# Batch 0 of an attention-and-mixer kernel: the w_tok2 matmuls read their moving operand contiguously, and the identity matmuls write PSUM with a step of four

## The chip, the cores and the metric

The kernel runs on one core of a Trainium2 chip. The metric is device time in microseconds: 292.88 us before the change, the median of three runs from 292.81 to 293.12. One further execution was profiled; it took 292.57 us, and the span in its trace, from the first to the last instruction, is 290.8 us. Its TensorE ran at a granted clock of 0.997.

## The reference

The inputs are eight batches of eight heads with 576 tokens of 64 values. A Performer attention comes first, then an MLP-mixer block on its output.

```python
# attention, per batch and head
phi(x) = exp(h - max(h)) / sqrt(128),  h = (x*scale) @ omega.T - |x*scale|^2 / 2
kv  = phi(k).T @ v ;  z = sum over tokens of phi(k)
x   = (phi(q) @ kv) / (phi(q) @ z + 1e-6)        # heads side by side: x is [576, 512]
# mixer, per batch
h   = relu(x.T @ w_tok1) @ w_tok2                # [512, 576], token mixing
u   = x + h.T                                    # [576, 512]
out = u + relu(u @ w_ch1) @ w_ch2                # channel mixing, d_ch = 1536
```

The sizes that matter below: w_tok2 is [256, 576], and of the 576 tokens of a batch the first 512 are handled apart from the last 64.

## The kernel before, in words

Everything is in fp16 in SBUF, with fp32 sums in PSUM. There are eight PSUM banks: six single ones, of which each step takes one or two (`bank`), and two used as a pair (`pair`). The 512 main tokens of a batch lie on 128 partitions by 4: token 4p + j is on partition p, at index j (`NJ` = 4). The last 64 tokens ("tails") are handled for two batches together.

For each batch the stages are: attention (`attention`, lines 498 to 719), which ends with VectorE dividing numerators by denominators into the tile x (L700, L701); token mixing; and channel mixing (`channel_mix`, L813 to L873), which runs 12 blocks of w_ch1 (L822), a relu on ScalarE (L839) and 12 blocks of w_ch2 for each of four groups of tokens (L855).

Channel mixing needs u with the features on partitions (`uT`). Batches 1 to 7 compute u with the tokens on partitions (`token_mix`, L721 to L758): w_tok2 is the stationary operand (L745), r1 the moving one, VectorE adds x (L748), and a DMA transposes the result (L753). Batch 0 has its own version, `token_mix_first` (L760 to L795), which gets uT straight from TensorE. For each of the four blocks of 128 features:

- L771 and L772 compute x.T @ w_tok1, ten matmuls of 128 columns, and a relu (L778 on ScalarE or L780 on VectorE) leaves r1.
- L787 runs four matmuls with x[:, j] as stationary operand and the identity as moving operand, which put the transposed x into the four quarters of one bank, quarter j holding the tokens 4c + j.
- L789 runs two matmuls of 512 columns on top, with r1 stationary and w_tok2 moving. `w2_of(tb)` gives w_tok2's columns in the order of these quarters: first all columns 4c, then all 4c + 1 and so on. So two neighbours in the stream are four fp16 values, 8 bytes, apart in SBUF.
- L793 casts the bank to fp16 into uT, on ScalarE for three blocks and on VectorE for one.

In batch 0 the residual u is added in channel mixing too: four identity matmuls with uT as stationary operand (L853) go between the w_ch2 matmuls. VectorE copies the sum to the fp32 tile `o` (L861), and SP stores it (L869), 128 rows of 2 KB, each fourth row of the batch's output.

The order of the work on each engine is written when the program is built. A planner (`Planner`) is given jobs, each with an engine, an assumed cost, a due key, its dependencies and the buffers it takes and gives; it plays them through and emits each engine's instructions in the order that comes out. Where TensorE would idle in the head of the kernel it puts in matmuls on zeros (L908). The head, up to about 28 us, holds batch 0's attention and token mixing; in it batch 1's k is transposed on TensorE as well (L465, L485), and the first feature maps of batch 1's keys follow (L611). Loads of batch 1 and of the weights are issued by POOL (L316, L334, L427 for w_ch1, L442 for w_ch2).

Of the kernel before, what the change touches and what calls it, by code (L numbers as in the profile page):

```python
# [37 lines left out]
class Planner:  # L38
# [20 lines left out]
    def add(self, eng, cost, key, fn, deps=(), take=(), give=(), rows=False, wire=0.0):  # L59
        job = Job(eng, cost, key, fn, [d for d in deps if d is not None], list(take), list(give), rows, wire)  # L60
        for g in job.give:
            self.left[g] = self.left.get(g, 0) + 1
        self.jobs.append(job)
        return job
# [108 lines left out]
    def place(self, tag, name):  # L173
        return self.held[tag, name]
# [3 lines left out]
def kernel(  # L178
# [12 lines left out]
    nc = tc.nc  # L191
# [6 lines left out]
    P = 128  # L198
    SM = 512
    ST = S - SM  # L200
    NJ = SM // P
    NT = DT // P
# [13 lines left out]
    def sb(shape, dt, name):  # L216
        return pool.tile(shape, dt, name=name)
# [14 lines left out]
    ident16 = sb([P, P], FP16, "ident16")  # L232
# [6 lines left out]
    w2 = sb([P, NT, S], FP16, "w2")  # L239
# [46 lines left out]
    def bank(name):  # L286
        return banks[place("bank", name)]
# [7 lines left out]
    def mm(n, cols):  # L295
        return n * (cols / 2400.0 + 0.0025)
# [7 lines left out]
    def dma(eng, key, wire, fn, deps=(), take=(), give=(), cost=None):  # L304
        cost = (0.75 if eng == "POOL" else 0.45) if cost is None else cost
        job = add(eng, cost, key, fn, deps, take, give, wire=wire)
        if eng == "POOL":
            job.after = issued[-1] if issued else None
            issued.append(job)
        return job  # L310
# [97 lines left out]
    def pads():  # L408
# [6 lines left out]
        out=w1m.rearrange("p j t -> p (j t)"), in_=moe_w_tok1[0:SM, :].rearrange("(p j) t -> p (j t)", j=NJ)))  # L415
# [2 lines left out]
        j_w1t.append(dma("POOL", key, 0.2, cost=0.58, fn=lambda: nc.gpsimd.dma_start(out=w1t[o * ST : (o + 1) * ST, o, :], in_=moe_w_tok1[SM:S, :]), deps=[j_w1tz]))  # L418
    load_w1t(0, HEAD["w1t"])
    j_w2 = dma("POOL", HEAD["w2"], 1.7, lambda: nc.gpsimd.dma_start(out=w2, in_=moe_w_tok2.rearrange("(i p) s -> p i s", p=P)))  # L420
    def w2_of(tb, j=None):
        rows = w2[:, tb, 0:SM].rearrange("p (c j) -> p j c", j=NJ)
        return rows if j is None else rows[:, j, :]
    j_wc1 = []
    def load_wc1(i):
        c0 = i * (DC // 2)
# [13 lines left out]
    for i in range(2):  # L440
        c0 = i * (NCB // 2)
        j_wc2.append(dma("POOL", -3.0 + 0.1 * i, 3.85, lambda c0=c0: nc.gpsimd.dma_start(  # L442
            out=wc2[:, c0 : c0 + NCB // 2, :], in_=moe_w_ch2[c0 * P : (c0 + NCB // 2) * P, :].rearrange("(i p) d -> p i d", p=P))))
# [3 lines left out]
        out=omega16.rearrange("p (i d) -> p i d", i=2), in0=omega_nat.unsqueeze(1).broadcast_to((P, 2, D)), scalar1=c_scale, scalar2=None, op0=ALU.mult), deps=j_om)  # L447
# [312 lines left out]
    def token_mix_first(b, key, step, jx):  # L760

        jrs, uT = [], []
        for db in range(ND):
            cols = slice(db * P, (db + 1) * P)
            n = ("h1", b, db)
            def t1(n=n, cols=cols):
                x = t_x[place("x", b)]
                for tb in range(NT):
                    ps = bank(n)[:, tb * P : (tb + 1) * P]
                    for j in range(NJ):  # L770
                        nc.tensor.matmul(ps, w1m[:, j, tb * P : (tb + 1) * P], x[:, j, cols], start=(j == 0), stop=False)  # L771
                    nc.tensor.matmul(ps, w1t[:, b % 2, tb * P : (tb + 1) * P], x[:, NJ, cols], start=False, stop=True)  # L772
            j1 = add("PE", mm(10, P), HEAD["t1"][db], t1, deps=[*jx[2 * db : 2 * db + 2], j_w1, j_w1t[b % 2]], take=[("bank", n), ("r1", b)])
            re_act, uo_act = BY["re"][db] == "A", BY["uo"][db] == "A"
            def relu(n=n, cols=cols, re_act=re_act):
                o, i = t_r1[place("r1", b)][:, :, cols], bank(n)[:, 0 : NT * P].rearrange("p (t c) -> p t c", t=NT)
                if re_act:
                    nc.scalar.activation(out=o, in_=i, func=AF.Relu)  # L778
                else:
                    nc.vector.tensor_relu(out=o, in_=i)  # L780
            jr = add("ACT" if re_act else "DVE", 0.3 if re_act else 0.38, HEAD["re"][db], relu, deps=[j1], give=[("bank", n)])
            jrs.append(jr)
            n2 = ("uT", b, db)
            def ut_(n2=n2, cols=cols):
                ps, x, r1 = bank(n2), t_x[place("x", b)], t_r1[place("r1", b)]
                for j in range(NJ):
                    nc.tensor.matmul(ps[:, j * P : (j + 1) * P], x[:, j, cols], ident16, start=(j == 0), stop=False, skip_group_check=True)  # L787
                for tb in range(NT):
                    nc.tensor.matmul(ps, r1[:, tb, cols], w2_of(tb), start=False, stop=(tb == NT - 1), skip_group_check=True)  # L789
            j2 = add("PE", mm(2, 512) + mm(4, P), HEAD["ut"][db], ut_, deps=[jr, j_w2, j_ident], take=[("bank", n2), ("uT", b)], give=[("x", b), ("r1", b)])  # L790
            def ut_out(db=db, n2=n2, uo_act=uo_act):
                o, ps = t_uT[place("uT", b)][:, :, db, :], bank(n2).rearrange("p (j c) -> p j c", j=NJ)
                (nc.scalar.copy if uo_act else nc.vector.tensor_copy)(out=o, in_=ps)  # L793
            uT.append(add("ACT" if uo_act else "DVE", 0.5 if uo_act else 0.69, HEAD["uo"][db], ut_out, deps=[j2], give=[("bank", n2)]))
        return jrs, uT  # L795
# [17 lines left out]
    def channel_mix(c, key, jt):  # L813
# [27 lines left out]
        for j in range(NJ):  # L841
            last = c == B and j == NJ - 1
            for hf in range(2 if last else 1):
                n = ("h4", c, j, hf)
                cols = slice(hf * (DM // 2), (hf + 1) * (DM // 2)) if last else slice(0, DM)
                prev = None
                for part in range(3):
                    def c2(j=j, part=part, n=n, cols=cols):
                        ps, r3 = bank(n), t_r3[place("r3", c)]
                        for cb in range(4 * part, 4 * part + 4):  # L850
                            if c == 0 and cb == NCB - 1:
                                for db in range(ND):
                                    nc.tensor.matmul(ps[:, db * P : (db + 1) * P], t_uT[place("uT", c)][:, j, db, :], ident16,  # L853
                                                     start=False, stop=False, skip_group_check=True)
                            nc.tensor.matmul(ps[:, cols], r3[:, cb, j * P : (j + 1) * P], wc2[:, cb, cols], start=(cb == 0), stop=(cb == NCB - 1))  # L855
                    prev = add("PE", mm(4, 256 if last else 512) + (mm(4, P) if c == 0 and part == 2 else 0.0), key + 0.5 + 0.5 * (3 * j + part) / 12 + 0.2 * hf, c2,
                               deps=[prev, *jr[4 * part : 4 * part + 4], *j_wc2], take=[("bank", n)], give=[("r3", c)] + ([("uT", c)] if c == 0 else []))
                k2 = key + 0.5 + 0.5 * (3 * j + 3) / 12
                def oadd(j=j, n=n, cols=cols):
                    if c == 0:  # L860
                        nc.vector.tensor_copy(out=t_o[place("o", (c, j))], in_=bank(n))  # L861
                        return
                    uu = t_u[place("u", c)][:, j, :] if c < B else ut[j]
                    nc.vector.tensor_tensor(out=t_o[place("o", (c, j))][:, cols], in0=uu[:, cols], in1=bank(n)[:, cols], op=ALU.add)  # L864
                jo = add("DVE", 0.4 if last else 0.69, k2, oadd, deps=[prev], take=[("o", (c, j))], give=[("bank", n)] + ([("u", c)] if 0 < c < B else []))
                def store(j=j, cols=cols, last=last):
                    o = t_o[place("o", (c, j))]
                    if c < B:
                        nc.sync.dma_start(out=out[c, 0:SM, :].rearrange("(p j) d -> p j d", j=NJ)[:, j, :], in_=o)  # L869
                    else:  # L870
                        for i in range(2):
                            (nc.scalar if j >= 2 and i else nc.sync).dma_start(out=out[2 * j + i, SM:S, cols], in_=o[i * ST : (i + 1) * ST, cols])
                dma("SP", k2, 0.65, store, deps=[jo], give=[("o", (c, j))], cost=0.4 if c < B else 0.8)  # L873

    for i in range(4):
# [65 lines left out]
```

The softmax here doesn't subtract the row's maximum and nothing guards it: scores larger than these inputs give would overflow.

## Time and profile before

| What | Before |
|---|---|
| Timed runs | 292.88 us (292.81 to 293.12) |
| Profiled span | 290.8 us |
| DVE (VectorE) busy | 145.3 us, 50% |
| ACT (ScalarE) busy | 155.9 us, 54% |
| POOL (GpSimd) busy | 90.6 us, 31% |
| L853, identity matmuls writing contiguously, duration | 219 ns |
| L793 on ScalarE, cast of one bank | 586 ns |
| Batch 0's stores L869, first issue | 59.8 us |

A page of the profile gives busy times of each engine, then the chain of work that ended last, followed back from the end of the kernel. The durations of single matmuls overlap, since the next one starts while the one before it drains: L853's 219 ns is the time from start to end of one matmul, while four of them in a row take 0.22 us in the chain. To price a matmul that is followed closely by others, the chain or the distance between starts is read. PEld is TensorE loading the stationary operand, which runs beside the matmul before it.

### The profile page before, as it was taken

How to read it: one execution, taken by the hardware profiler on the slowest of the kernel's cores; microseconds unless marked ns; L12 is line 12 of the kernel's file. 1: busy time of each engine (PE TensorE's matmuls, PEld its weight loads, DVE VectorE, ACT ScalarE, POOL GpSimd, SP SyncE). 2: the span in 40 equal slices, each digit the busy share in tenths (PEclk: the TensorE clock that was granted, in tenths of full speed). 3: DMA queues.
4: the chain of work that ended last, by engine and by line, in shares of the span. 5: the costliest groups of instructions: out<-in, count | busy, mean ns of one | idle time of the engine just before them, and what ended most of it. 6: DMA issues, size and time to landing. Idle time of an engine off the chain costs nothing.

```text
span 290.8 us, 5502 instructions
## 1 busy us (share of the span) xinstructions
PE 283.9 (98%) x2210; PEld 141.7 (49%) x2210; DVE 145.3 (50%) x269; ACT 155.9 (54%) x305; POOL 90.6 (31%) x115
## 2 busy tenths in 40 slices
PE   7899999999999999999999999999999999999994
PEld 3465454445544544465445544554455444444443
DVE  4885843558449533756567446646465242111011
ACT  5963992098457553865466636753765501621700
POOL 8995740128006501550165014601421000000000
PEclk9999999999999999999999999999999999999998
DMA  8999999699964996999769976897711033003004
GB/s 192 193 197 195 202 228 172 98 246 175 177 108 108 186 152 125 180 171 202 113 129 182 197 114 113 159 221 115 152 72 39 0 72 147 0 18 144 2 20 124
DMA packets 75737, 39.57 MB, mean 136 GB/s; under 512 B 54976, under 2 KB 70720, under 8 KB 75328
## 3 DMA queue, kind: packets, MB, share of 16 engines
q0 software_dynamic: 24304, 17.43, 41.2%
q1 hardware_dynamic: 50624, 21.01, 32.3%
q10 hardware_dynamic: 784, 0.79, 0.9%
q8 instruction: 17, 0.28, 0.4%
q14 instruction: 8, 0.07, 0.1%
HBM read 35.88 MB, written 16.52 MB: 180 GB/s over the span
## 4 chain that ended last, share of the span: by engine, by line
PE 95%; ACT 3%; DVE 0%; issue 0%; DVEq 0%; ACTq 0%
PE bank L855 33%; PE bank L822 32%; PE bank L745 4%; PE bank L728 4%; PE bank L611 3%; PE bank L657 3%; PE bank L625 2%; PE pair L691 2%; PE bank L908 2%; ACT kp L494 1%; PE bank L789 1%; PE bank L803 1%; PE bank L664 1%; PE bank L465 1%; PE bank L729 1%; ACT qp L494 1%
## 5 line engine op out<-in xcount | busy, mean ns | idle before, releaser
L839 ACT ACTIVATE r<-bank 128x512 f16<-128x512 f32 x108 | 64.5, 602 | 69.8 <-PE bank L822 69.8
L855 PE MATMUL bank<-wc,r 128*128 128x512 f16 (+1 forms) x444 | 101.5, 374 | 0.0
L822 PE MATMUL bank<-uT,wc 128*128 128x512 f16 x376 | 89.5, 379 | 0.0
L855 PEld LDWEIGHTS <-r 128*128 128x128 f16 x444 | 40.8, 98 | 46.9 <-issue 5.1
L822 PEld LDWEIGHTS <-wc 128*128 128x128 f16 x424 | 39.5, 98 | 42.6 <-issue 0.5
L637 DVE TENSOR_REDUCE km<-kp 128x8 f16<-128x1024 f16 x32 | 38.7, 1209 | 9.4 <-ACT kp L494 9.2
L494 ACT ACTIVATE qp<-bank 128x512 f16<-128x512 f32 x64 | 35.2, 620 | 13.4 <-PE bank L625 13.4
L494 ACT ACTIVATE kp<-bank 128x512 f16<-128x512 f32 x64 | 34.4, 610 | 8.9 <-PE bank L611 8.9
L644 POOL TENSOR_TENSOR vs<-v,vs 128x512 f16<-128x512 f16 x32 | 33.4, 1055 | 16.1 <-DVE vs L639 12.1
L864 DVE TENSOR_TENSOR o<-u,bank 128x512 f32<-128x512 f16 x28 | 19.1, 681 | 28.1 <-PE bank L855 28.1
L571 POOL TENSOR_TENSOR vbd<-vt,vbd 128x1024 f16<-128x1024 f16 x7 | 13.4, 1919 | 33.2 <-DVE vbd L562 21.7
L365 POOL COPY ktt<-kT 128x256 f16<-128x256 f16 x6 | 2.4, 396 | 68.4 <-DMA kT<-k 68.4
L701 DVE TENSOR_TENSOR x<-pair,rc 128x640 f16<-128x640 f32 x28 | 23.1, 824 | 1.0
L748 DVE TENSOR_TENSOR u<-x,bank 128x512 f16<-128x512 f16 x28 | 17.4, 682 | 9.1 <-PE bank L745 9.1
L700 DVE RECIPROCAL rc<-pair 128x10 f32<-128x10 f32 x28 | 6.0, 216 | 26.9 <-PE pair L693 26.9
L691 PEld LDWEIGHTS <-qp 128*128 128x128 f16 x256 | 12.8, 98 | 6.1 <-issue 0.7
L736 DVE TENSOR_SCALAR r<-bank 128x512 f16<-128x512 f32 x7 | 4.8, 692 | 19.5 <-PE bank L729 19.5
L728 PE MATMUL bank<-x,w1m 128*128 128x512 f16 x56 | 14.4, 379 | 0.0
L657 PEld LDWEIGHTS <-kp 128*128 128x128 f16 x256 | 10.9, 98 | 5.3 <-ACT qp L494 0.9
L657 PE MATMUL bank<-vs,kp 128*128 128x65 f16 x256 | 13.0, 193 | 0.4 <-ACT qp L494 0.4
L745 PE MATMUL bank<-r,w 128*128 128x512 f16 x56 | 13.2, 379 | 0.0
L611 PE MATMUL bank<-omT,kT 64*128 64x128 f16 x256 | 12.5, 218 | 0.1
(102 smaller groups left out, 267.8 us busy)
## 6 DMA issues: line engine op xcount, KB each, us to landing
out_dram<-o SPq DMA_DIRECT2D x32, 256.0 KB, 2.5
q<-in_q_dram POOLq DMA_DIRECT2D x6, 576.0 KB, 6.5
k<-in_k_dram POOLq DMA_DIRECT2D x6, 576.0 KB, 10.2
wc<-in_moe_w_ch_dram POOLq DMA_DIRECT2D x4, 768.0 KB, 10.3
v<-in_v_dram POOLq DMA_DIRECT2D x6, 512.0 KB, 6.3
r<-in_q_dram POOLq DMA_DIRECT2D x4, 256.0 KB, 7.2
v<-in_v_dram POOLq DMA_DIRECT2D x4, 256.0 KB, 7.2
out_dram<-o SPq DMA_DIRECT2D x5, 128.0 KB, 2.3
```

What stands on the lines that cost most here:

```text
L494: nc.scalar.activation(out=out, in_=in_, func=AF.Exp, bias=0.0, scale=1.0)
L611: nc.tensor.matmul(ps[e][:, c : c + M], m[half[e], r, :], omT[half[e]], start=True, stop=True)
L637: nc.vector.reduce_max(out=mx, in_=kpv, axis=AX.X)
L644: nc.gpsimd.tensor_tensor(out=vs[:, :, 0:D], in0=t_v[place("v", b)][:, hh[0] : hh[0] + 2, :].rearrange("p h (j d) -> p (h j) d", d=D), in1 ...
L657: nc.tensor.matmul(ps[:, i, :], kpv[:, 2 * i + j // 2, j % 2, :], vs[:, i * NJ + j, 0 : D + 1], start=(i == 0 and j == 0), stop=False, ski ...
L701: nc.vector.tensor_tensor(out=t_x[place("x", b)][:, :, (2 * hp + hs[0]) * D : (2 * hp + hs[0] + n) * D].rearrange("p j (i d) -> p i j d", ...
L728: nc.tensor.matmul(ps, w1m[:, j, tb * P : (tb + 1) * P], x[:, j, :], start=(j == 0), stop=False)
L745: nc.tensor.matmul(ps, w2_of(tb, j), r1[:, tb, :], start=(tb == 0), stop=(tb == NT - 1))
L822: nc.tensor.matmul(ps, wc1[:, db, cb * P : (cb + 1) * P], moving(db), start=(db == 0), stop=(db == ND - 1))
L839: nc.scalar.activation(out=t_r3[place("r3", c)][:, cb, :], in_=bank(n), func=AF.Relu)
L855: nc.tensor.matmul(ps[:, cols], r3[:, cb, j * P : (j + 1) * P], wc2[:, cb, cols], start=(cb == 0), stop=(cb == NCB - 1))
L864: nc.vector.tensor_tensor(out=t_o[place("o", (c, j))][:, cols], in0=uu[:, cols], in1=bank(n)[:, cols], op=ALU.add)
```

## The change

Batch 0's uT is computed with its tokens in natural order. The identity matmul for group j now writes to every fourth column of the bank, beginning at column j, so that token 4c + j lands in column 4c + j. The w_tok2 matmuls then take the first 512 columns of w_tok2 as they lie in SBUF. The cast reads the bank as before, so uT's quarter j now holds the tokens 128j to 128j + 127, and batch 0's stores write 128 neighbouring rows each. The other batches are as they were; `w2_of` is left with its use as a stationary operand there.

```diff
-    def w2_of(tb, j=None):
-        rows = w2[:, tb, 0:SM].rearrange("p (c j) -> p j c", j=NJ)
-        return rows if j is None else rows[:, j, :]
+    def w2_of(tb, j):
+        return w2[:, tb, 0:SM].rearrange("p (c j) -> p j c", j=NJ)[:, j, :]
...
                 for j in range(NJ):
-                    nc.tensor.matmul(ps[:, j * P : (j + 1) * P], x[:, j, cols], ident16, start=(j == 0), stop=False, skip_group_check=True)
+                    nc.tensor.matmul(ps.rearrange("p (c j) -> p j c", j=NJ)[:, j, :], x[:, j, cols], ident16, start=(j == 0), stop=False, skip_group_check=True)
                 for tb in range(NT):
-                    nc.tensor.matmul(ps, r1[:, tb, cols], w2_of(tb), start=False, stop=(tb == NT - 1), skip_group_check=True)
+                    nc.tensor.matmul(ps, r1[:, tb, cols], w2[:, tb, 0:SM], start=False, stop=(tb == NT - 1), skip_group_check=True)
...
                     if c < B:
-                        nc.sync.dma_start(out=out[c, 0:SM, :].rearrange("(p j) d -> p j d", j=NJ)[:, j, :], in_=o)
+                        rows = out[c, 0:SM, :]
+                        rows = rows.rearrange("(p j) d -> p j d", j=NJ)[:, j, :] if c else rows[j * P : (j + 1) * P, :]
+                        nc.sync.dma_start(out=rows, in_=o)
```

## The prediction, made before the changed kernel ran

> **What bounds the kernel now.** I read the page first (busy times, then the chain), then the lines of the changed matmuls, then the chain in order of time from 17 to 29 us, then the timeline there, and last the landings of the transfers behind it.
>
> ```profile
> span 290.8 us, 5502 instructions
> ...
> PE 283.9 (98%) x2210; PEld 141.7 (49%) x2210; DVE 145.3 (50%) x269; ACT 155.9 (54%) x305; POOL 90.6 (31%) x115
> ...
> PE 95%; ACT 3%; DVE 0%; issue 0%; DVEq 0%; ACTq 0%
> ```
>
> TensorE is the bound: it carries 95% of the chain that ended last. After about 17 us it shows no wait for another engine. So time taken out of TensorE's stream after that shortens the kernel, unless an operand arrives too late. The lines of the changed matmuls, and of the same operations in other places:
>
> ```profile
> L789 PE MATMUL bank<-w,r x8: 612/621/632, 19.9 to 27.0; 128*128 128x512 f16 x8
> L787 PE MATMUL bank<-ident,x x16: 218/219/219, 19.7 to 26.5; 128*128 128x128 f16 x16
> L745 PE MATMUL bank<-r,w x56: 379/379/379, 52.0 to 233.0; 128*128 128x512 f16 x56
> ```
>
> The columns are minimum, median and maximum ns. L789 is the matmul that streams w_tok2 with a step of four columns: 621 ns, where L745 (same size, streaming contiguous r1) takes 379. These durations overlap each other, so the price is taken from the chain, which gives start, duration and work with the overlap removed:
>
> ```profile
> 19.82 0.22 PE bank L787 x4
> 20.04 0.90 PE bank L789 x2
> 20.94 0.12 PE bank L691 x4
> ...
> 22.80 0.22 PE bank L787 x4
> 23.02 0.90 PE bank L789 x2
> 23.92 0.23 PE bank L771 x4
> ...
> 24.48 0.22 PE bank L787 x4
> 24.70 0.90 PE bank L789 x2
> 25.61 0.90 PE bank L465 x16
> 26.50 0.22 PE bank L787 x4
> 26.73 0.90 PE bank L789 x2
> 27.63 0.13 PE bank L485
> ```
>
> All four column blocks of batch 0 are on the chain: two strided matmuls cost 0.90 us (0.45 each), four identity matmuls 0.22 (0.055 each). A contiguous 512-column matmul costs 0.216 here: twelve L855 from 45.43 take 2.59 us.
>
> **What the Trainium skill says.** "TensorE: Matmul & The Clock Gate", section "Back-to-back issue gap", gives N/2.4 + 2.5 ns for a warm gap: 216 ns at 512 columns, 56 at 128. The trace agrees (0.216, 0.055). "SBUF — State Buffer", section "Door 1: The DMA port swizzle" (its note on cachelines), says that two hits on a 16-byte line are enough for full rate. A step of 8 bytes gives two, yet the trace shows 0.45 against 0.216; the measurement decides. "PSUM — Partial Sum Buffer", section "Specifications (TRN2)", says PSUM lines are 8 bytes and that a non-contiguous pattern "slows matmuls significantly", without a factor. No matmul in this trace writes PSUM with a step, so nothing here confirms it. It is the open price of this change.
>
> **The change part by part.** I compared the order and the waits of every instruction on all engines, before and after: they are the same. The planner's costs are unchanged, so this is a change of access patterns alone.
>
> 1. *w_tok2 contiguous.* 8 matmuls go from 0.45 to 0.216 us: 8 x 0.234 = 1.87 us off TensorE, 0.47 per block. This is as sure as anything here, since operand, size and destination are those of an ordinary 512-column matmul.
>
> 2. *Identity matmuls write PSUM with a step of four.* 16 matmuls of 128 columns, 0.055 us each now. Bounds: no stretch (nothing added), since a write need not behave as a read does; fourfold (each written column costs as much as four), 16 x 0.165 = 2.64 us. Below nothing is excluded: no access gets more compact. I take the ratio of the strided read, 0.45/0.216 = 2.08, because with 8-byte lines a step of four floats leaves one useful float in a line instead of two, which also gives a factor of two. That is 0.115 us each, 16 x 0.06 = 0.95 us, 0.24 per block. It is an estimate from another operation, and both ends are kept.
>
> 3. *The cast out of PSUM (L793)* reads the same shape, contiguous, before and after: nothing. *The four stores of batch 0 (L869)* move the same 256 KB in 2 KB rows, now side by side in DRAM. They are issued from 59.8 us on SP and land 2.9 to 3.1 us later; the output ring has four buffers and the next batch's stores come after 70 us. Hidden behind channel mixing either way.
>
> The blocks can't all hand on what they save. The third block's first matmuls (L771 at 22.08) need two head outputs from VectorE, which works without a gap from 20.52 to 23.12 and isn't moved by the change:
>
> ```profile
> 21.38 0.49 DVE L701 TENSOR_TENSOR x<-bank,rc 128x320 f16<-128x320 f32 x1
> ...
> 21.64 0.59 PE L908 MATMUL bank<-zeros 128*128 128x512 f16 x2
> ...
> 22.08 0.39 PE L771 MATMUL bank<-x,w1m 128*128 128x128 f16 x4
> ```
>
> That VectorE operation ends at 21.87. The first block's L771 started 0.05 us after its own (L701 ended at 18.08, matmul at 18.13), so this one can go at about 21.93: at most 0.15 us earlier, whatever the first block saved. (L908 is filler that keeps TensorE busy.) The fourth block's L771 (23.74) needs the L701 that ends at 23.12, so it can gain at most 0.57. The third and fourth identity-and-w2 groups follow without such a limit: their relus (L780 ends at 23.45, L778 at 24.90) come before.
>
> Sum with factor two: a block saves 0.47 - 0.24 = 0.23; the first hands on 0.15, the others 0.23 each: 0.15 + 3 x 0.23 = 0.84 us. With no stretch: 0.15 + 0.42 (second, limited to 0.57 in all) + 0.47 + 0.47 = 1.51 us.
>
> From 28 us on, does everything else keep pace? ScalarE is busy for 8.00 of the 8 us from 28 to 36, but its work is released by these same matmuls and by its own cast (L793, which waited 1.4 us for TensorE at the last block), so it shifts along. Transfers issued by POOL keep their times. The tightest are the second half of batch 1's q, issued at 24.22, landing 8.7 later at 32.9, used at 35.91; and w_ch2's second half, issued at 28.56, landing 13.7 later at 42.3, used at 45.27. Both leave 3 us, more than the gain. Later loads are released by work that shifts too.
>
> So 290.8 - 0.84 = 290.0 us for the profiled span; it lies 1.8 us under the timed 292.57 of the same execution, and the timed runs have their median at 292.88. The forecast is 292.88 - 0.84 = 292.0.
>
> **Rivals.**
> - *The strided write costs nothing.* For it: [...]no row shows a penalty. Against it: the strided read doubled. Gain 1.51: 291.4 us.
> - *The gain is taken back by a later wait, or the stretch is about threefold.* A wait would have to appear at TensorE between 28 and 60 us, on VectorE (POOL's vs), ScalarE or a transfer. For it: the transfers are dense until 45 us and ScalarE is full. Against it: the 3 us of slack above. Threefold: 16 x 0.11 = 1.76 against 1.87. Either gives 292.6 to 292.9.
> - *Slower: the strided write costs fourfold.* Each block then adds 0.66 and saves 0.47, 0.19 more in each of four: +0.77, 293.6 us. It decides from 0.055 + 1.87/16 = 0.172 us for an identity matmul, about 3.1 times today's. For it: the page's "significantly", and these matmuls lead into accumulation in the same bank. Against it: a fourfold price needs more than one access for each column.
>
> **How the numbers follow.** Factor about two 0.45 (292.0; own range 291.8 to 292.4), no stretch 0.21 (291.4), taken back or threefold 0.21 (292.8), fourfold 0.13 (293.6). A difference of 0.2% is 0.59 us, about what a measurement of this kernel can tell from no change. The first two cases end beyond it except for a sliver of the first (a factor of 2.3 would do): faster 0.65. Same 0.23, from the third case and that sliver; slower 0.12. The range of 291.1 to 293.2 holds the first three cases with the spread of the runs, and leaves out the fourfold case and some tails.
>
> **What would show it.** Step 1: the w2 matmuls at 379 ns like L745, 0.43 for two in the chain. Step 2: the identity matmuls' duration over 219 ns, and in the chain four taking 0.22 (no stretch), about 0.46 (factor two) or 0.88 (fourfold). The VectorE limit: L771 of the third block at about 21.9, with a short gap before it on TensorE. Keeping pace: L855's first batch near 44.4 instead of 45.27, and the same lead at the end. A w2 matmul still over 500 ns, a lead at 28 us that is gone at 60 us, or four identity matmuls over 0.7 us would make the forecast wrong.

## The result, and the profile after

The changed kernel takes 291.83 us (median of four runs, 291.68 to 291.89) against 292.85 for the kernel before (four runs, the three of the table and one more); the ratio is 0.9964, 95% interval 0.9946 to 0.9981. Run again later beside other kernels it gave 0.9972 (0.9964 to 0.9980). The forecast was 292.0.

From the edit to `w2_of` down to the stores, the lines of the program carry a number lower by one: L786 are the identity matmuls, L788 the w2 matmuls, L770 the x.T @ w_tok1 matmuls, L792 the cast. From the stores on, the number is higher by one: the filler L908 is L909. The busy times of the page have hardly moved. They come first, then the two lines of the changed matmuls:

```profile
span 290.1 us, 5502 instructions
...
PE 282.9 (98%) x2210; PEld 142.4 (49%) x2210; DVE 145.3 (50%) x269; ACT 155.8 (54%) x305; POOL 90.7 (31%) x115
```

```profile
L788 PE MATMUL bank<-w,r x8: 379/400/421, 20.3 to 26.6; 128*128 128x512 f16 x8
L786 PE MATMUL bank<-ident,x x16: 272/314/314, 19.9 to 26.2; 128*128 128x128 f16 x16
```

The median duration of a w2 matmul fell from 621 to 400 ns, and that of an identity matmul rose from 219 to 314. The chain in order of time (start, duration, work) gives the two prices:

```profile
18.39 0.38 PE bank L770 x4
...
20.07 0.44 PE bank L786 x4
20.51 0.43 PE bank L788 x2
20.94 0.12 PE bank L690 x4
...
22.24 0.32 PE bank L770 x4
...
26.52 0.43 PE bank L788 x2
26.95 0.13 PE bank L484
...
27.39 0.75 PE bank L827 x3
```

Two w2 matmuls take 0.43 us instead of 0.90, four identity matmuls 0.44 instead of 0.22, which is twice. The third block's L770 takes 0.32 here, where four such matmuls take 0.22 elsewhere: the 0.1 us is the wait for VectorE. On the timeline this L770 starts 0.06 us after the division that it needs:

```profile
21.63 0.49 DVE L700 TENSOR_TENSOR x<-bank,rc 128x320 f16<-128x320 f32 x1
...
22.18 0.38 PE L770 MATMUL bank<-x,w1m 128*128 128x128 f16 x4
```

In this execution the head of the kernel happened to run later: the first block starts at 18.39 us instead of 18.13. This start differs from one execution to the next: it lies between 18.02 and 18.66 in all the profiles of this document, and another profile of the changed kernel has it at 18.08. So the stretch from there to the first matmul of channel mixing (L828 before, L827 after) is the better measure. These are its ends before:

```profile
18.13 0.38 PE bank L771 x4
...
28.07 0.75 PE bank L828 x3
```

Before it is 28.07 - 18.13 = 9.94 us; after, 27.39 - 18.39 = 9.00. The change saves 0.94 us there, and the head gives 0.26 back in this one execution. The lead stays to the end: channel mixing begins 0.68 us earlier, and the last 60 w_ch2 matmuls begin at 275.87 in the chain instead of 276.52, 0.65 earlier.

### The profile page after: what moved, and what is told of

It reads as the page before. It is cut to its first block, busy times and chain, and to the rows that moved or that the text cites. A ratio compares the mean times of both kernels' runs of the same rounds, so it can differ in the third digit from the quotient of the medians.

```text
span 290.1 us, 5502 instructions
## 1 busy us (share of the span) xinstructions
PE 282.9 (98%) x2210; PEld 142.4 (49%) x2210; DVE 145.3 (50%) x269; ACT 155.8 (54%) x305; POOL 90.7 (31%) x115
## 4 chain that ended last, share of the span: by engine, by line
PE 94%; ACT 3%; DMA 1%; DVE 0%; issue 0%; DVEq 0%; ACTq 0%
PE bank L854 33%; PE bank L821 32%; PE bank L744 4%; PE bank L727 4%; PE bank L610 3%; PE bank L656 3%; PE bank L624 2%; PE pair L690 2%; ACT kp L493 1%; PE bank L802 1%; PE bank L663 1%; PE bank L464 1%; PE bank L728 1%; DMA omega_nat<-in_omega_dram 1%; ACT qp L493 1%; PE bank L909 1%
```

## The experiments

Each time below is a median beside runs of the kernel before on the same chip (292.8 to 292.9 us), with the ratio to it.

**The two halves by themselves.** `e1_w2_only` is the kernel before with only this edit:

```diff
-  nc.tensor.matmul(ps, r1[:, tb, cols], w2_of(tb), ...)
+  nc.tensor.matmul(ps, r1[:, tb, cols], w2[:, tb, 0:SM], ...)
```

> The kernel before with step 1 alone: w_tok2 streams contiguously, the identity matmuls still write contiguously. It leaves out the match of the two token orders in batch 0, so x is added to the wrong tokens there. My theory (two independent prices and a limit set by VectorE): two w2 matmuls 0.43 us in the chain, four identity matmuls 0.22, the third block's first matmul held by VectorE's division to within 0.1 us of its end, and 1.5 us less than before: 291.4 us. Rival (the gain of the head is taken back by a later wait once it is over 1 us): about the same time as the changed kernel, 291.8, with a wait on TensorE between 28 and 60 us. Rival (the w2 matmuls were slow because of what stood beside them, not because of their step): still 0.9 for two, 292.9.

Measured: 291.41 us, 0.9949 (0.9936 to 0.9961). Its chain at the third block:

```profile
20.20 0.22 PE bank L787 x4
20.42 0.43 PE bank L789 x2
...
21.72 0.55 PE bank L908 x2
22.27 0.03 issue
22.30 0.38 PE bank L771 x4
```

The w2 matmuls are fast by themselves, so their price was their step. The stretch from the first block to channel mixing is 26.92 - 18.52 = 8.40 us, 1.54 less than before, although four blocks saved 4 x 0.47 = 1.88. What is missing is lost at the third block, where it was looked for, in two pieces. The filler L908 takes 0.55 instead of 0.43, since it starts 0.12 us later behind the matmul ahead of it: at 21.67, 0.05 us after a division (start 21.13, duration 0.49) is done at 21.62, which probably released its bank. Then TensorE stands until the next division (start 21.76, duration 0.49) is done at 22.25; L771 starts at 22.30.

`e2_step_only` is the kernel before with only the identity matmuls' edit:

```diff
-  nc.tensor.matmul(ps[:, j * P : (j + 1) * P], x[:, j, cols], ident16, ...)
+  nc.tensor.matmul(ps.rearrange("p (c j) -> p j c", j=NJ)[:, j, :], x[:, j, cols], ident16, ...)
```

> The kernel before with step 2 alone: the identity matmuls write PSUM with a step of four, w_tok2 still streams with a step of four columns. It leaves out the match of the two token orders in batch 0. My theory: four identity matmuls take 0.44 us in the chain, each of the four blocks costs 0.22 more and TensorE has nothing to hide it behind: 0.9 us more, 293.75 us. Rival (the longer write is partly hidden by waits on VectorE in the head): 293.2 to 293.4.

Measured: 293.76 us, 1.0029 (1.0019 to 1.0040). Its chain at the first block:

```profile
20.35 0.44 PE bank L787 x4
20.78 0.88 PE bank L789 x2
```

Four identity matmuls take 0.44 and two w2 matmuls 0.88, a little less than the 0.90 of before; why they do is not shown. The stretch is 29.37 - 18.66 = 10.71 us, 0.77 more than before: about 4 x (0.22 - 0.02). So the identity's step, which looks like a detail of the change, takes back nearly half of what the contiguous read brings in a block (0.22 of 0.47), and nothing in the head hides it.

**The stores.** `e3_old_stores` is the changed kernel with batch 0's rows going to every fourth row again:

```diff
-  rows = rows.rearrange("(p j) d -> p j d", j=NJ)[:, j, :] if c else rows[j * P : (j + 1) * P, :]
+  rows = rows.rearrange("(p j) d -> p j d", j=NJ)[:, j, :]
```

> The changed kernel with batch 0's stores going to every fourth row again, as before the change; so batch 0's rows land in another order than the reference's. My theory (the stores are hidden): same time as the changed kernel, 291.8 us. Rival (part of the gain comes from the contiguous rows): over 292.1 us.

Measured: 291.85 us, 0.9968 (0.9956 to 0.9979). The stretch is 9.00 us, as in the changed kernel, and the ratio is the changed kernel's within the intervals: the stores' order is worth nothing that can be told from the noise.

**What the price of a step is.** `p1_ladder` gives each of the four blocks of the kernel before its own pattern of writes and reads:

```diff
+  # identity writes: step 3 | step 2 | runs of 4 | runs of 2
+  ps[:, 0:384].rearrange("p (c r) -> p r c", r=3)[:, j % 3, :]                          # block 0
+  ps[:, (j // 2) * 256 : (j // 2 + 1) * 256].rearrange("p (c r) -> p r c", r=2)[:, j % 2, :]  # block 1
+  ps.rearrange("p (c j r) -> p j c r", j=4, r=4)[:, j]                                  # block 2
+  ps.rearrange("p (c j r) -> p j c r", j=4, r=2)[:, j]                                  # block 3
+  # w2 reads: step 8 "p (c j) -> p j c", j=8 | step 2, j=2 | runs of 4, r=4 | runs of 2, r=2
```

> Prices alone; batch 0's token order is given up (x and the mixed part land on wrong tokens). Each of the four blocks of the kernel before writes and reads in another pattern. Writes of the four identity matmuls: block 0 step three floats, block 1 step two, block 2 runs of four floats, block 3 runs of two floats (8 bytes) with a gap of six. Reads of the two w2 matmuls: block 0 step eight columns (16 bytes), block 1 step two (4 bytes), block 2 runs of four columns (8 bytes), block 3 runs of two columns (4 bytes) with a gap. My theory (TensorE takes and gives columns in neighbouring pairs; a column without its neighbour costs a whole slot): writes 0.44 us per four for steps two and three, 0.22 for runs of two and four; reads 0.9 per two for steps two and eight, 0.43 for runs of two and four. Rival (the price grows with the step): step two of the writes near 0.3, step eight of the reads well over 0.9, step two of the reads near 0.43. Rival (any pattern that is not contiguous pays): 0.44 and 0.9 for the runs too.

The diff is abbreviated: for the runs, the identity is regrouped to the shape of what is written as well, and its columns stay in order. There is one execution, of 293.16 us. Here is its chain, where L791, L789, L793 and L795 are the writes with step two, step three, runs of four and runs of two, and L801, L799, L803 and L805 are the reads with step two, step eight, runs of four and runs of two:

```profile
19.94 0.44 PE bank L791 x4
20.37 0.45 PE bank L801 x2
...
22.76 0.44 PE bank L789 x4
23.19 1.78 PE bank L799 x2
...
25.53 0.22 PE bank L793 x4
25.75 0.46 PE bank L803 x2
...
27.11 0.22 PE bank L795 x4
27.33 0.90 PE bank L805 x2
```

With step four from the kernels before and after, the patterns stand like this:

| Pattern | Four identity writes | Columns in an 8-byte line | Two w2 reads | Columns in a 16-byte line |
|---|---|---|---|---|
| contiguous | 0.22 us | 2 | 0.43 us | 8 |
| runs of four | 0.22 | 2 | 0.46 | 4 |
| runs of two | 0.22 | 2 | 0.90 | 2 |
| step two | 0.44 | 1 | 0.45 | 4 |
| step three | 0.44 | 1 | not run | - |
| step four | 0.44 | 1 | 0.90 | 2 |
| step eight | not run | - | 1.78 | 1 |

For the writes my theory held: a pair of neighbouring floats is the unit, a float without its neighbour costs a slot of its own, and a step of three or four costs no more than one of two. All pairs that were run begin at an even float, so pairs that lie across two lines are not priced. For the reads the theory fell. I had expected pairs there too, so 0.9 for steps two and eight; they took 0.45 and 1.78, and runs of two, expected at 0.43, took 0.90. What fits all six read patterns is a 16-byte line as the unit: nearly full speed (0.43 to 0.46) with four or more fp16 columns used of each line, twice the time with two, four times with one. A unit of 8 bytes would give step two and runs of two the same price, and one of 32 bytes would do so for step four and runs of four; neither is so.

**Using it.** If only the lines count, a layout exists that is free on both sides. Token 8c + 4r + j goes to column 8c + 2j + r: the identity matmuls write pairs, and the w2 matmuls read the eight columns of each 16-byte line one after the other, out of order. `g2_pairs_cast` is the changed kernel with this (abbreviated, the identity regrouped as above):

```diff
-  ps.rearrange("p (c j) -> p j c", j=NJ)[:, j, :]
+  ps.rearrange("p (c j r) -> p j c r", j=NJ, r=2)[:, j]            # identity matmuls
-  w2[:, tb, 0:SM]
+  w2[:, tb, 0:SM].rearrange("p (c r j) -> p c j r", j=NJ, r=2)     # w2 matmuls
+  # the cast reads "p (q c j r)" and writes "p q (c r j)": natural order in uT
```

> A layout that should cost TensorE nothing on either side and needs no copy of w_tok2: token 8c + 4r + j goes to column 8c + 2j + r of the bank. The identity matmuls write runs of two floats (8 bytes) with gaps; the w2 matmuls read all eight fp16 columns of one 16-byte stretch one after the other, in the order 0, 4, 1, 5, 2, 6, 3, 7; the cast out of PSUM puts them in natural order, so the stores are the changed kernel's. My theory (the price is the number of 8-byte lines written or 16-byte lines read, and the order within a line is free): four identity matmuls 0.22, two w2 matmuls 0.43 to 0.46, and 291.4 us as with e1_w2_only and f1_w2_copy, if the cast with its steps is not longer than 1 us. Rival (reads out of order pay, each jump a slot): w2 still 0.9 for two, 292.9 us.

Measured: 291.19 us, 0.9946 (0.9934 to 0.9958). It is the lowest median here, though its interval doesn't tell it from the other kernels without a price on either side. The chain at the third block:

```profile
22.40 0.38 PE bank L770 x4
...
23.12 0.22 PE bank L786 x4
23.34 0.43 PE bank L788 x2
```

Both prices are those of contiguous operands, so this order within a line costs nothing. The cast stays at 585 ns on ScalarE and 692 on VectorE although it reads every second float of PSUM in turn (586 and 691 before). The stretch is 27.02 - 18.61 = 8.41 us, as in `e1_w2_only`.

`g1_pairs` is the same with the cast as it was, and two stores of 64 rows each in place of one of 128.

> The same layout, but with the cast as it was; batch 0's rows then lie in the bank's order, and its stores put them in place, two of 64 rows instead of each one of 128. My theory: 291.4 us again, the four more stores on SP being hidden behind channel mixing. Rival (the longer SP queue delays batch 3's transposes): over 291.7 us.

Measured: 291.32 us, 0.9957 (0.9945 to 0.9970): no loss from the extra stores that can be told from the noise. `after_again` ran beside the two.

> The changed kernel once more, beside the other two on the same chip: 291.85 us, 0.4 us above the pair layouts by my theory, no difference by the rival that a wait for batch 1's transpose takes back what goes beyond 1 us.

Measured: 292.08 us, 0.9972 (0.9964 to 0.9980), 0.9 us above `g2_pairs_cast` and 0.8 above `g1_pairs`. That is more than the 0.4 us expected, and more than the 0.6 us between their stretches (9.00 against 8.41). Of the changed kernel's 22 runs here, 20 lie between 291.5 and 292.7, so the 0.3 us over is within their spread.

**The other way to be contiguous.** `f1_w2_copy` is the kernel before with a permuted copy of w_tok2 in SBUF (abbreviated):

```diff
+  w2p = sb([P, NT, SM], FP16, "w2p")
+  add("DVE" / "ACT", 0.6, -2.5, copy w2_of(tb) into w2p[:, tb, :], deps=[j_w2])   # tb = 0 / 1
-  nc.tensor.matmul(ps, r1[:, tb, cols], w2_of(tb), ...)
+  nc.tensor.matmul(ps, r1[:, tb, cols], w2p[:, tb, :], ...)
```

> Neither step costs anything on TensorE: the kernel before with one permuted copy of w_tok2's main part in SBUF, made once by VectorE (first 128 rows) and ScalarE (the others) before the first block needs it, so both the identity writes and the w2 reads are contiguous, in the old token order and with the old stores. My theory: as e1_w2_only, 1.5 us less than before, 291.4 us, if the two copies of about 0.6 us fall into the 0.76 us that each of these engines waits at about 18.2 us. Rival (the copies push VectorE's divisions back, which limit the third block): gain reduced by up to 0.5 us, 291.6 to 291.9 us.

Measured: 291.48 us, 0.9950 (0.9936 to 0.9964). The copies took 0.57 us on VectorE and 0.71 on ScalarE and fell into those engines' waits at 18 us; the stretch is 26.60 - 18.20 = 8.40 us again. But TensorE's waits in its profiled execution show something new:

```profile
PE bank L825 <- DMA uT<-u: 0.8, 1, 0.8
```

And its chain runs through the transfer:

```profile
53.64 9.41 DMA uT<-u
63.05 0.05 issue
63.10 4.49 PE bank L825 x20
```

The first matmul of batch 1's channel mixing stood for a transpose of u, which was issued at 53.64 us and took 9.4 to land, at 63.0; before, it was issued at 55.11, took 6.7 and landed at 61.8, 1.9 us ahead of its use. Beside it runs POOL's load of batch 2's v, issued at 53.82 (before, 53.49), which follows the arrival of batch 2's k and not the pace of TensorE. So a TensorE that is ahead brings the transpose's issue close to that load. How long the transpose then takes differs: in `e1_w2_only`, `g1_pairs` and `g2_pairs_cast`, whose stretch is the same, it took 8.4, 8.4 and 7.7 us and landed 0.2 to 0.9 ahead of its use. `f2_copy_early_v` and `a2_after_early_v` move that load ahead, in `f1_w2_copy` and in the changed kernel:

```diff
-  load_v(b, b + key_of("lv", b), [ld["ktt", b]])
+  load_v(b, b + key_of("lv", b), [ld["ktt", b]] if b > NPE else [])
```

> f1_w2_copy with one more edit: POOL issues the load of batch 2's v after batch 1's scaling of v instead of after the tail copy of batch 2's k, so it does not share the DMA engines with batch 1's transpose of u. My theory (in f1_w2_copy the transpose landed so late, at 63.0 us, that TensorE waited 0.85 us for it, beside the v load): the transpose lands below 61 us, no wait before batch 1's channel mixing, 291.2 us and a smaller spread of the runs. Rival (the transpose is slow of itself, or the load now delays batch 2's k): as f1_w2_copy, 291.5.

> The changed kernel with that same earlier load of batch 2's v. My theory: in the changed kernel the transpose lands just in time (63.0 us, where channel mixing starts), so its wait takes less than 0.1 us: 291.8 us as the changed kernel. Rival (in most runs the late transpose takes part of the gain): 291.5 us or less.

Measured: 291.43 us, 0.9955 (0.9942 to 0.9968), and 291.98 us, 0.9973 (0.9965 to 0.9981). The transpose now lands 4.6 and 4.5 us after its issue, and neither profile has a wait for it. So the load beside it was what made it slow, and not batch 0's stores, which run beside it too and stay. Yet neither kernel is faster than its own base (291.48, and 291.83 or 292.08). For the changed kernel this was expected: its transpose landed at 63.0, just as it was needed. For `f1_w2_copy` the lead over the kernel before tells where time was lost in the profiled execution: 1.47 us at the start of batch 0's channel mixing, 0.58 at the last 60 w_ch2 matmuls. With the earlier load it is 1.29 and 1.18, so this edit gave back 0.1 us in this execution, in which batch 2's k arrived at 57.0 instead of 53.4. In all the other profiles of this document the lead stays the same within 0.06 us. And the five kernels with this stretch have medians from 291.19 to 291.48, which leaves no room for a wait of 0.85 us in the middle runs of `f1_w2_copy`. So the wait looks rare; how often it comes is not shown, since only one of its executions has a trace.

## Why the prediction was right

- *w_tok2 contiguous.* Forecast: 0.47 us saved for each block. Measured 0.47 (0.90 to 0.43), with and without the other step.
- *The identity's step.* Forecast from the strided read: 2.08 times, 0.115 us each. Measured 2.0 times, 0.11. The value was right, but one of its two reasons was not. That the strided read has the same ratio is a coincidence, and taking the size from it was luck: the reads fit 16-byte lines and the writes 8-byte lines, and step four happens to cost twice in both, while step two costs nothing in a read (0.45) and twice in a write (0.44). The other reason, one useful float in an 8-byte line instead of two, is what the ladder shows. The rivals of no stretch, threefold and fourfold are out by the measured 0.44.
- *The VectorE limit.* Forecast: the third block can gain at most 0.15 us. In the changed kernel its L770 starts 3.79 us after the first block's on the timeline, 3.95 before, so 0.16 was handed on. In `e1_w2_only` the limit cost 0.34 us of 1.88, with 0.37 forecast.
- *The sum.* Forecast 0.84, measured 0.94 in the stretch and 1.0 between the medians; 1.51 forecast and 1.54 measured with no stretch of the writes. Most of the 0.1 us is the identity term, 0.22 for each block instead of 0.24: 0.16 + 3 x (0.47 - 0.22) = 0.91.
- *Keeping pace.* Right for the changed kernel, but in part by luck. The tightest transfer was batch 1's transpose of u, with 1.9 us of slack, which the forecast did not list, while it named 3 us as the smallest. "Later loads are released by work that shifts too" does not hold for what runs beside it: the transpose's issue shifted along, by 0.68 us, but batch 2's v load came 1.1 us later in this execution (54.61 instead of 53.49), and the transpose landed 1.2 us later. That used up the slack and no more; in the profile of `after_again` 0.5 us of it was left.
- *The stores and the cast* were worth nothing, as forecast. The landings were misread: 2.9 to 3.1 us does not hold for all four stores, the fourth takes 8.5 before (issued at 64.85), and the four take 5.9 to 9.5 after. Nothing on TensorE waits for them.

"SBUF — State Buffer", section "Door 1: The DMA port swizzle", asks for two hits on a 16-byte line for full rate; for a moving operand in fp16 the ladder shows 0.90 us with two and 0.45 with four, so here the measurement decides. "PSUM — Partial Sum Buffer", section "Specifications (TRN2)", says that any non-contiguous pattern slows a matmul; the 8-byte line that it names is borne out, but runs of two floats with gaps took 0.22 us, the contiguous price.

## What to carry to other kernels

Price a matmul's access pattern in lines and not in steps: 16 bytes of the moving operand, of which at least four fp16 columns must be used (0.45 us against 0.90 with two), and 8 bytes of PSUM, of which both floats must be used (0.22 against 0.44). When a permutation has to go somewhere, split it so that each side stays within its lines, as the pair layout does, instead of giving one side the whole stride. And when TensorE gets ahead, list the transfers that don't move with it, and what runs beside them, as well as those with little slack.

## What the runs showed of the hardware that was not expected

- A moving operand's step of two fp16 columns costs nothing (0.45 us for two 512-column matmuls against 0.43), a step of eight four times (1.78). The one other order within a 16-byte line that was run (0, 4, 1, 5, 2, 6, 3, 7) costs nothing either (0.43).
- A matmul's write with a step of two, three or four floats costs twice (0.44 us for four of 128 columns against 0.22), and runs of two floats with gaps nothing (0.22).
- ScalarE and VectorE cast a PSUM bank in the same time whether they read it contiguously or every second float in turn (586 and 585 ns on ScalarE, 691 and 692 on VectorE).
- A transpose by DMA took 6.7 to 9.4 us beside a load of 512 KB, and 4.5 or 4.6 with that load moved ahead.
